# The last stage of an adaLN transformer block: seven block products, three of them 512 columns wide, four accumulated in two banks

## Chip, cores and metric

The kernel runs on one core of a Trainium2 chip. The metric is the device time of one execution in microseconds, as the median of several runs; lower is better.

## What is computed

`x` is 2048 tokens of width D = 512 in float32. The block is a linear-attention layer followed by a bilinear feed-forward layer, each with a layer norm that is scaled and shifted from a conditioning vector. Only the last line of the feed-forward layer is touched by the change.

```python
mod = (silu(c) @ w_mod)                       # sa, ca, ga, sb, cb, gb
h = layernorm(x) * (1 + ca) + sa
x = x + ga * linear_attention(h, wqkv) @ wo   # 32 heads of 16
h = layernorm(x) * (1 + cb) + sb
g = h @ w_gate                                # 512 -> 1376
u = h @ w_up
x = x + gb * ((g * u) @ w_down)               # 1376 -> 512
```

## The kernel before, in words

**Tiles and precision.** Tokens lie in four chunks of 512 (chunk c is `xts[c]`, four tiles of 128 tokens, `j` = 0 to 3). The 1376 features lie in ten tiles of 128 rows and one odd tile of 96. Every float32 operand of a matmul is split in a high part (rounded to the matmul's format, on ScalarE) and a low part (the difference, mostly on VectorE), and a product takes three matmuls: high by high, high by low, low by high.

**The feed-forward layer for chunks 2 and 3.** The generator `ffn` first runs eight gate blocks for chunks 0 and 1 and then eleven for chunks 2 and 3, one per feature tile (order `LATE`: the odd tile first). A gate block (`block`) is seven block products of six 512-column matmuls each (line 1156). Between them stand points named p1, p5, p6, p2, p7, p3, p4, in this order, and a plan (`put(b, point, ...)`) hangs other work on a point of block `m + b`. Block 3 of this numbering begins at 403.49 us in the profile below. Blocks from the fourth on alternate between two sets of four PSUM banks, `banks` and `others`; the last one uses `banks`.

**The last stage.** `Down.run` multiplies the hidden values of chunks 2 and 3 by `w_down`. The ten full feature tiles form five pairs (A, B), and each pair is a 2 by 2 block product done with seven multiplications: a11 and a21 are the hidden values of A for chunks c0 = 2 and c1 = 3, a12 and a22 those of B; b11 and b12 are the left and the right 256 columns of `w_down` for A, b21 and b22 for B. `w_sum` makes t1 to t4 from the b blocks, `h_sum` makes s1 to s4 from the a blocks (s1 = a21 + a22, s3 = a11 - a21, s2 = s1 - a11, s4 = a12 - s2), `h_split` and `h_next` split them. The seven products are a11 b11, s1 t1, a12 b21, s2 t2, s4 b22, s3 t3 and a22 t4. Each goes over all five pairs and over the four token tiles `j`.

The weights are split during the gate blocks, written to DRAM (`w_park`), and fetched again (`w_fetch`, line 1398, on SyncE's DMA queue, five loads of 256 KB for each product). A split weight is one tile of 128 x 2 x 256: high columns, then low columns. The odd feature tile takes no part in the seven products: its 96 rows are added as a plain product of its own, wherever a bank for that output is open.

**What sets the order.** It is written out by hand: each engine executes its instructions in the order in which `run` issues them. SyncE's queue is in order too, so a load that waits for a buffer holds up the loads behind it. All SBUF tiles of 2 KB per partition come from one pool of 94 buffers; `drop` gives the tiles of a finished product back.

**Banks before.** A product is 256 columns wide, so two token tiles share a bank, and a product takes two banks: X = `others[:2]`, Z = `others[2:]`, Y = `banks[:2]`, O = `banks[2:]`. X takes a11 b11; ScalarE copies it to Y (two copies); a12 b21 is then accumulated in X, s2 t2, s3 t3 and a22 t4 in Y, s1 t1 and s4 b22 in Z. `add` lets VectorE add a finished bank to the tokens (line 1503); a bank that is accumulated further is read, not cleared. The products run in halves of two token tiles (`lo`, `hi`), with the preparation of a later product between the halves. The odd tile's right columns for c1 are a short product of their own in O before the last one.

Of the kernel before, what the change touches and what calls it, by code (L numbers as in the profile page):

```python
# [11 lines left out]
ALU = mybir.AluOpType  # L12
AX = mybir.AxisListType

P = 128
# [9 lines left out]
def tile_adaln_block(  # L25
# [12 lines left out]
    nc = tc.nc  # L38
# [4 lines left out]
    NJ = 4  # L43
# [33 lines left out]
    def B(tag, shape=(P, D), dt=F32):  # L77

        return T(tiles, tag, shape, dt)
# [1261 lines left out]

    HALF = D // 2

    FOLLOWS = {"s2": "s4"}

    class Down:

# [59 lines left out]
        def h_sum(self, name, *pairs):  # L1407
            for i in pairs:
                x, y, alu = {"s1": ("a21", "a22", ALU.add), "s3": ("a11", "a21", ALU.subtract),
                             "s2": ("s1", "a11", ALU.subtract), "s4": ("a12", "s2", ALU.subtract)}[name]  # L1410
                own = self.parts.setdefault(i, {})
                x, y = self.a(i, x), self.a(i, y)
                to = {"s1": lambda: B("s"), "s3": lambda: y, "s2": lambda: x, "s4": lambda: x}[name]()
                own[name] = to
                nc.vector.tensor_tensor(to, x, y, op=alu)

# [17 lines left out]
        def ahead(self, name, i):  # L1434
            if name and name not in self.parts[i]:
                self.h_sum(name, i)

        def part(self, bs, j):
            return bs[j // 2][:, j % 2 * HALF:(j % 2 + 1) * HALF]

        def mm(self, bs, j, pairs, start):
# [3 lines left out]
            for n, ((h, l), w) in enumerate(pairs):  # L1445
                k = h.shape[0]
                for x, y in ((h, w[:k, 0]), (h, w[:k, 1]), (l, w[:k, 0])):
                    nc.tensor.matmul(ps, x[:, a:b], y, start=start, stop=False, skip_group_check=True)  # L1448
                    start = False

        def product(self, bs, js, left, right, start, odd=None):
            pairs = [(self.parts[i][left, "split"], self.w[right, i]) for i in range(self.NI)]
            if odd:
                pairs.append((self.h[LATE[0]][odd[0]], self.w["odd", odd[1]]))
            for j in js:
                self.mm(bs, j, pairs, start and j % 2 == 0)

        def drop(self, left, right):
            for i in range(self.NI):
# [2 lines left out]
        def planned(self):  # L1462

            def put(b, point, *does):
                plan.setdefault((self.m + b, point), []).extend(does)

            put(1, "p6", lambda: nc.vector.tensor_tensor(self.odd, self.odd, gb[:self.odd.shape[0]], op=ALU.mult))
            put(1, "p4", *(lambda n=n: self.w_split(("odd", n), self.odd[:, n * HALF:(n + 1) * HALF], nc.gpsimd) for n in range(2)))
            for i in range(self.NI):
                a, b = 1 + 2 * i, 2 + 2 * i  # L1470
                put(a - 1, "p4", lambda i=i: self.w_load(i))
# [15 lines left out]
                if i + 1 < self.NI:  # L1487
                    put(b + 1, "p1", lambda i=i: self.w_park(i, "t2", "t3", "t4"))
                    put(b + 1, "p5", lambda i=i: self.h_sum("s1", i))
                    put(b + 1, "p6", lambda i=i: self.h_sum("s3", i))  # L1490
                else:
                    put(b, "p3", lambda: self.w_fetch("b11"))
                    put(b, "p4", lambda i=i: self.w_park(i, "t2", "t3", "t4"), lambda: self.w_fetch("t1"))

        def run(self):

            c0, c1 = self.cs
            x = lambda c, half, j: xts[c][j][:, half * HALF:(half + 1) * HALF]
            X, Z, Y, O = others[:2], others[2:], banks[:2], banks[2:]

            def add(c, half, bs, js, store=None):
                for j in js:
                    nc.vector.tensor_tensor(x(c, half, j), x(c, half, j), self.part(bs, j), op=ALU.add)
                    if store:
                        a, b = store
                        nc.sync.dma_start(ov[c, j, :, a:b], xts[c][j][:, a:b])

            lo, hi = (0, 1), (2, 3)
            last = self.NI - 1
            self.h_sum("s1", last)  # L1510
            self.h_split("s1", *range(self.NI))
            self.w_fetch("b21")
            self.product(X, lo, "a11", "b11", True)
            copy(Y[0], X[0])
            self.h_split("a12", 0, 1)
            self.product(X, hi, "a11", "b11", True)
            self.h_split("a12", 2)
            copy(Y[1], X[1])
            self.drop("a11", "b11")
            self.h_sum("s3", last)  # L1520
            self.h_split("a12", 3, 4)
            self.w_fetch("t2")
            self.product(Z, lo, "s1", "t1", True)
            self.h_next("s2", 0, 1)
            add(c1, 1, Z, lo)
            self.product(Z, hi, "s1", "t1", True)
            self.h_next("s2", 2, 3)
            add(c1, 1, Z, hi)
            self.drop("s1", "t1")
            self.w_fetch("b22")  # L1530
            self.product(X, lo, "a12", "b21", False, (0, 0))
            self.h_next("s2", 4)
            self.h_next("s4", 0)
            add(c0, 0, X, lo)
            self.product(X, hi, "a12", "b21", False, (0, 0))
            self.h_next("s4", 1, 2)
            add(c0, 0, X, hi)
            self.drop("a12", "b21")
            self.w_fetch("t3")
            self.product(Y, lo, "s2", "t2", False)  # L1540
            self.h_next("s4", 3, 4)
            add(c0, 1, Y, lo)
            self.product(Y, hi, "s2", "t2", False)
            self.h_split("s3", 0, 1)
            add(c0, 1, Y, hi)
            self.drop("s2", "t2")
            self.w_fetch("t4")
            self.product(Z, lo, "s4", "b22", False, (0, 1))
            self.h_split("s3", 2, 3, 4)
            add(c0, 1, Z, lo, (0, D))  # L1550
            self.product(Z, hi, "s4", "b22", False, (0, 1))
            self.h_split("a22", 0, 1)
            add(c0, 1, Z, hi, (0, D))
            self.drop("s4", "b22")
            self.product(Y, lo, "s3", "t3", False)
            self.h_split("a22", 2, 3)
            add(c1, 1, Y, lo)
            self.product(Y, hi, "s3", "t3", False)
            self.h_split("a22", 4)
            add(c1, 1, Y, hi)  # L1560
            self.drop("s3", "t3")
            odd = [(self.h[LATE[0]][1], self.w["odd", 1])]
            for j in range(NJ):
                self.mm(O, j, odd, j % 2 == 0)
            add(c1, 1, O, range(NJ), (HALF, D))
# [5 lines left out]
            add(c1, 0, Y, before, (0, HALF))  # L1571

    def fill(n):
        for _ in range(n):
# [263 lines left out]
```

## Time and profile before

| | |
|---|---|
| median of 3 runs | 541.37 us (541.33 to 541.59) |
| the profiled execution | 541.17 us, of which the span from the first to the last instruction is 539.5 us |
| TensorE | 533.7 us busy, 99% of the span |
| VectorE, ScalarE, GpSimd | 75%, 55%, 30% |
| last stage (479.5 to 535.7 us) | TensorE 56.20 of 56.20 us busy, VectorE 36.59, ScalarE 15.94, GpSimd 0; granted TensorE clock 1.00 |
| after the last matmul | one add on VectorE, one store of 128 KB |

The profile is one execution. In it, a matmul's record begins when the matmul starts and ends by a model, so records overlap and the distance from one start to the next is what a matmul costs; "PEld" is the loading of a matmul's stationary weights, which has records of its own. In this kernel each matmul has its own load. "L1448 PE" names a line of the program and the engine. The chain of waits is followed back from the last instruction.

### The profile page before, as it was taken

To read this page: it belongs to the slowest core of one execution; us is meant where nothing else is said; L and a number is where in the kernel's file an instruction comes from. 1 tells how busy PE (TensorE), PEld (TensorE's weight loads), DVE (VectorE), ACT (ScalarE), POOL (GpSimd) and SP (SyncE) were. 2 spreads that over 40 slices of the span, in tenths; PEclk is the share of its full clock that TensorE was granted. 3 is DMA by queue.
4 is the path that set the end of the run, shared out by engine and by line. 5 is a ranking of instruction groups with operands and counts; after the bars stand their busy time and mean duration, and the time that the engine had idled before them with its cause. 6 is when DMAs were issued, how large, how long until landed. Compare 5 with 4: busy or idle time off the path is not lost.

```text
span 539.5 us, 8146 instructions
## 1 busy us (share of the span) xinstructions
PE 533.7 (99%) x2617; PEld 447.8 (83%) x2617; DVE 402.6 (75%) x688; ACT 295.8 (55%) x557; POOL 159.5 (30%) x169
## 2 busy tenths in 40 slices
PE   8999999999999999999999999999999999999997
PEld 6888787888888878878888888887888888899997
DVE  7997779999989888779766576996555564669742
ACT  3696777648587764577684545454434334264500
POOL 2001010010021220076696577747532313210000
PEclk9999999999999999999999999999999999999999
DMA  8913426220165165947879596793289998689222
GB/s 279 386 37 102 133 94 219 88 69 2 37 203 187 47 207 145 311 138 225 283 208 320 194 329 217 223 378 105 81 297 346 393 393 305 221 300 346 91 80 78
DMA packets 86394, 109.20 MB, mean 202 GB/s; under 512 B 10896, under 2 KB 41616, under 8 KB 86352
## 3 DMA queue, kind: packets, MB, share of 16 engines
q1 hardware_dynamic: 86352, 108.70, 59.6%
q8 instruction: 20, 0.33, 0.2%
q14 instruction: 22, 0.18, 0.1%
HBM read 65.93 MB, written 42.73 MB: 201 GB/s over the span
## 4 chain that ended last, share of the span: by engine, by line
PE 94%; DVE 3%; SPq 1%; issue 1%; DMA 0%; ACT 0%; DVEq 0%
PE bank L1156 27%; PE acc L873 8%; PE acc L1156 7%; PE acc L1448 6%; PE bank L1448 5%; PE bank L211 4%; PE bank L209 3%; PE bank L210 3%; PE acc L1239 3%; PE acc L1240 3%; PE acc L1241 3%; PE acc L416 2%; PE acc L418 2%; PE bank L956 2%; PE bank L958 2%; PE acc L417 2%
## 5 line engine op out<-in xcount | busy, mean ns | idle before, releaser
L1156 PE MATMUL bank<-h,w 128*128 128x512 f32 (+1 forms) x630 | 145.3, 389 | 0.0
L1156 PEld LDWEIGHTS bank<-h,w 128*128 128x128 f32 (+1 forms) x630 | 117.1, 186 | 25.9
L1161 ACT ACTIVATE bank<-bank 128x512 f32<-128x512 f32 (+1 forms) x30 | 17.5, 584 | 74.5 <-PE bank L1156 74.4
L197 DVE TENSOR_TENSOR kl<-u,kh 128x512 fp32r<-128x512 f32 (+1 forms) x38 | 26.5, 735 | 25.4 <-ACT kh L196 23.3
L265 POOL TENSOR_TENSOR rstd<-ve,half 128x2 f32<-128x2 f32 (+3 forms) x13 | 11.8, 910 | 108.6 <-DVE ve L264 44.0
L211 PE MATMUL bank<-w,h 128*128 128x512 f32 x104 | 40.9, 393 | 0.1
L209 PE MATMUL bank<-w,h 128*128 128x512 f32 x104 | 40.9, 393 | 0.0
L210 PE MATMUL bank<-w,h 128*128 128x512 f32 x104 | 40.5, 390 | 0.0
L1156 PE MATMUL acc<-h,w 128*128 128x512 f32 x168 | 38.7, 389 | 0.0
L197 POOL TENSOR_TENSOR w<-raw,w 128x512 fp32r<-128x512 f32 (+1 forms) x15 | 22.1, 1479 | 53.4 <-ACT w L196 47.8
L873 PE MATMUL acc<-w,xh 128*128 128x512 f32 x120 | 37.1, 390 | 0.0
L1156 PEld LDWEIGHTS acc<-h,w 128*128 128x128 f32 x168 | 31.5, 188 | 6.5
L943 DVE TENSOR_TENSOR x<-acc,x 128x512 f32<-128x512 f32 x40 | 26.5, 686 | 12.8 <-PE acc L1241 11.1
L1118 POOL TENSOR_TENSOR w<-raw,w 128x256 fp32r<-128x256 f32 (+3 forms) x22 | 24.4, 1108 | 37.8 <-ACT w L1111 33.6
L1448 PE MATMUL acc<-w,kh 128*128 128x256 f32 (+1 forms) x176 | 31.8, 283 | 0.0
L1118 POOL TENSOR_TENSOR w<-t,w 128x512 fp32r<-128x512 f32 (+1 forms) x22 | 29.7, 1350 | 0.0
L1448 PEld LDWEIGHTS acc<-w,kh 128*128 128x128 f32 (+1 forms) x176 | 27.5, 192 | 0.1
L873 PEld LDWEIGHTS acc<-w,xh 128*128 128x128 f32 x120 | 22.5, 188 | 4.6
L416 PE MATMUL acc<-kh,xh 128*128 128x512 f32 x64 | 25.2, 394 | 0.0
L418 PE MATMUL acc<-kl,xh 128*128 128x512 f32 x64 | 25.0, 391 | 0.0
L417 PE MATMUL acc<-kh,xl 128*128 128x512 f32 x64 | 25.0, 390 | 0.0
L1239 PE MATMUL acc<-w,kh 128*128 128x512 f32 x64 | 24.9, 389 | 0.0
(261 smaller groups left out, 1325.8 us busy)
## 6 DMA issues: line engine op xcount, KB each, us to landing
right<-w SPq DMA_DIRECT2D x56, 256.0 KB, 3.5
w<-right SPq DMA_DIRECT2D x56, 256.0 KB, 5.1
raw<-in_w_mod_dram SPq DMA_DIRECT2D x24, 256.0 KB, 3.8
raw<-in_B_w_down_dram SPq DMA_DIRECT2D x20, 256.0 KB, 3.8
down_t<-w SPq DMA_DIRECT2D x20, 256.0 KB, 5.0
w<-down_t SPq DMA_DIRECT2D x20, 256.0 KB, 4.6
x<-in_A_x_dram SPq DMA_DIRECT2D x16, 256.0 KB, 5.4
down_b<-w SPq DMA_DIRECT2D x15, 256.0 KB, 5.1
```

The source lines that it names most:

```text
L197: (low or nc.vector).tensor_tensor(l, src, f32(h), op=ALU.subtract)
L209: nc.tensor.matmul(ps, ah, bh, start=i == 0, stop=False)
L210: nc.tensor.matmul(ps, ah, bl, start=False, stop=False)
L211: nc.tensor.matmul(ps, al, bh, start=False, stop=i == n - 1)
L416: nc.tensor.matmul(tacc[k], xh[:, a:b], kh, start=first, stop=False)
L417: nc.tensor.matmul(tacc[k], xl[:, a:b], kh, start=False, stop=False)
L418: nc.tensor.matmul(tacc[k], xh[:, a:b], kl, start=False, stop=last)
L873: nc.tensor.matmul(yps[i], x, y, start=False, stop=k == KD - 1 and x is al, skip_group_check=True)
L1118: sub = lambda out, x, y: (on or nc.gpsimd).tensor_tensor(out, x, f32(y), op=ALU.subtract)
L1156: mm = lambda x, y, **kw: nc.tensor.matmul(ps, x[:, k], y, skip_group_check=True, **kw)
L1239: nc.tensor.matmul(ps, hh[:, a:b], dh[:n, c:d], start=i == 0, stop=False)
L1448: nc.tensor.matmul(ps, x[:, a:b], y, start=start, stop=False, skip_group_check=True)
```

## The change

In the last stage, products are now of two kinds. **Wide**: a12 b21, s1 t1 and s4 b22 use all four banks A = `banks`, one per token tile. The high part of `a` is multiplied by the weight's high and low columns side by side, 512 columns in one matmul, and the low part by the high 256 columns, which are accumulated on the left half of the bank: two matmuls where there were three. VectorE then adds the left and the right half of each bank to the tokens. **Narrow**: a11 b11, s2 t2, s3 t3 and a22 t4 are accumulated one after the other in C = `others[:2]`, 256 columns at a time as before, and VectorE adds the running sum to another quarter of the output after each. The two copies from X to Y are gone.

The two kinds alternate: a11 b11 (C), a12 b21 (A), s2 t2 (C), s1 t1 (A), s3 t3 (C), s4 b22 (A), a22 t4 (C). Products run whole, no longer in halves. The odd tile's right columns for c1 are put into the chain with s3 t3; since they then also stand in what follows, the last product adds the odd tile with its left minus its right columns. `odd_turn`, at point p5 of block 3, makes this difference in place (a VectorE subtraction, a ScalarE copy, a GpSimd subtraction, each 96 x 256). s2 is now written over a11 and not over s1, which is split later; s1's and s3's last sums both stand before the first product.

```diff
-    FOLLOWS = {"s2": "s4"}
+    FOLLOWS = {}
...
-                to = {"s1": lambda: B("s"), "s3": lambda: y, "s2": lambda: x, "s4": lambda: x}[name]()
+                to = {"s1": lambda: B("s"), "s3": lambda: y, "s2": lambda: y, "s4": lambda: x}[name]()
...
+        def odd_turn(self):
+            x = self.odd
+            nc.vector.tensor_tensor(x[:, :HALF], x[:, :HALF], x[:, HALF:], op=ALU.subtract)
+            self.w_split(("odd", "turn"), x[:, :HALF], nc.gpsimd)
...
+        def mm_wide(self, bs, j, pairs, start):
+
+            a, b = j * P, (j + 1) * P
+            for (h, l), w in pairs:
+                k = h.shape[0]
+                nc.tensor.matmul(bs[j], h[:, a:b], w[:k].rearrange("p t c -> p (t c)"), start=start, stop=False, skip_group_check=True)
+                nc.tensor.matmul(bs[j][:, :HALF], l[:, a:b], w[:k, 0], start=False, stop=False, skip_group_check=True)
+                start = False
...
+            put(3, "p5", self.odd_turn)
...
-                    put(b, "p4", lambda i=i: self.w_park(i, "t2", "t3", "t4"), lambda: self.w_fetch("t1"))
+                    put(b, "p4", lambda i=i: self.w_park(i, "t2", "t3", "t4"), lambda: self.w_fetch("b21"))
...
+            A, C = banks, others[:2]
...
-                    nc.vector.tensor_tensor(x(c, half, j), x(c, half, j), self.part(bs, j), op=ALU.add)
+                    parts = [bs[j][:, :HALF], bs[j][:, HALF:]] if bs is A else [self.part(bs, j)]
+                    for ps in parts:
+                        nc.vector.tensor_tensor(x(c, half, j), x(c, half, j), ps, op=ALU.add)
...
+            self.h_sum("s1", last)
+            self.h_sum("s3", last)
+            self.h_split("a12", *pairs)
+            self.w_fetch("t2")
+            self.product(C, js, "a11", "b11", True)
+            self.drop("a11", "b11")
+            self.h_next("s2", 0, 1)
+            add(c0, 0, C, js)
+            self.w_fetch("t1")
+            self.product(A, js, "a12", "b21", True, (0, 0))
+            self.drop("a12", "b21")
+            self.h_next("s2", 2, 3, 4)
+            add(c0, 0, A, js)
+            self.w_fetch("t3")
+            self.product(C, js, "s2", "t2", False)
+            self.drop("s2", "t2")
+            self.h_split("s1", *pairs)
+            add(c0, 1, C, js)
+            self.w_fetch("b22")
+            self.product(A, js, "s1", "t1", True)
+            self.drop("s1", "t1")
+            self.h_split("s3", *pairs)
+            self.h_next("s4", 0)
+            add(c1, 1, A, js)
+            self.w_fetch("t4")
+            self.product(C, js, "s3", "t3", False, (1, 1))
+            self.drop("s3", "t3")
+            self.h_next("s4", 1, 2, 3, 4)
+            add(c1, 1, C, js, (HALF, D))
+            self.product(A, js, "s4", "b22", False, (0, 1))
+            self.drop("s4", "b22")
+            self.h_split("a22", *pairs)
+            add(c0, 1, A, js, (0, D))
...
-                self.product(Y, (j,), "a22", "t4", False, (1, 0))
-                add(c1, 0, Y, before, (0, HALF))
+                self.product(C, (j,), "a22", "t4", False, (1, "turn"))
+                add(c1, 0, C, before, (0, HALF))
```

**Order on TensorE, at the end of the stage's first product.** In the program before, the second product is s1 t1 in Z (`acc_4525`); `w` is a weight tile, `kh` and `kl` the high and low part of a hidden value (here the stationary operand is the hidden value, whatever the order of the names); x2 is two matmuls that read alike, by the high and by the low columns.

```order
L1448 MATMUL acc_4524<-w_5254,kh_5199 128x256 x2
L1448 MATMUL acc_4524<-w_5254,kl_5200 128x256
L1448 MATMUL acc_4525<-w_5269,kh_5281 128x256 x2
L1448 MATMUL acc_4525<-w_5269,kl_5282 128x256
L1448 MATMUL acc_4525<-w_5271,kh_5285 128x256 x2
L1448 MATMUL acc_4525<-w_5271,kl_5286 128x256
```

The same place in the changed program; the second product is a12 b21 in A (`bank_2865` for the first token tile).

```order
L1453 MATMUL acc_4524<-w_5258,kh_5203 128x256 x2
L1453 MATMUL acc_4524<-w_5258,kl_5204 128x256
L1461 MATMUL bank_2865<-w_5273,kh_5286 128x512
L1462 MATMUL bank_2865<-w_5273,kl_5287 128x256
L1461 MATMUL bank_2865<-w_5275,kh_5290 128x512
L1462 MATMUL bank_2865<-w_5275,kl_5291 128x256
```

The first product is as before; in the second, each group of three matmuls of 256 columns has become one of 512 and one of 256.

**Order on SyncE's DMA queue, at the start of the stage.** These are the loads for the second and the third product before: t1, then b21 (the number behind the block's name is the pair).

```order
L1398 DMA w_1113_5271<-down_t1_1_4682 128x512
L1398 DMA w_1114_5273<-down_t1_2_4868 128x512
L1398 DMA w_1115_5275<-down_t1_3_5054 128x512
L1398 DMA w_1116_5277<-down_t1_4_5226 128x512
L1398 DMA w_1128_5301<-down_b21_0_4495 128x512
L1398 DMA w_1129_5303<-down_b21_1_4645 128x512
```

And in the changed program, at the same places of the queue:

```order
L1398 DMA w_1114_5275<-down_b21_1_4649 128x512
L1398 DMA w_1115_5277<-down_b21_2_4835 128x512
L1398 DMA w_1116_5279<-down_b21_3_5021 128x512
L1398 DMA w_1117_5281<-down_b21_4_5193 128x512
L1398 DMA w_1129_5306<-down_t2_0_4548 128x512
L1398 DMA w_1130_5308<-down_t2_1_4738 128x512
```

The loads are as many and as large; their order is now b21, t2, t1, t3, b22, t4, the order in which the products need them, where it was t1, b21, t2, b22, t3, t4.

**Order on VectorE, between the last gate block and the second product.** Before: the last multiplication of the gate block (L1184), the last s1 sum (L1415), then the low parts of s1 (L197, `kl`).

```order
L1184 TENSOR_TENSOR u_5197<-bank_2867,u_5197 128x512
L1415 TENSOR_TENSOR s_5279<-u_5120,u_5197 128x512
L197 TENSOR_TENSOR kl_5282<-s_4564,kh_5281 128x512
L197 TENSOR_TENSOR kl_5286<-s_4750,kh_5285 128x512
L197 TENSOR_TENSOR kl_5290<-s_4936,kh_5289 128x512
```

After: the last s3 sum stands there too, and the low parts are those of a12.

```order
L1184 TENSOR_TENSOR u_5201<-bank_2867,u_5201 128x512
L1415 TENSOR_TENSOR s_5283<-u_5124,u_5201 128x512
L1415 TENSOR_TENSOR u_5124<-u_5135,u_5124 128x512
L197 TENSOR_TENSOR kl_5287<-u_4442,kh_5286 128x512
L197 TENSOR_TENSOR kl_5291<-u_4670,kh_5290 128x512
```

The five low parts that the second product needs moved back by one sum.

More of the change, by code (lines that the diff above doesn't have):

```diff
@@ L1455, in product @@
             for j in js:
-                self.mm(bs, j, pairs, start and j % 2 == 0)
+                if len(bs) == NJ:
+                    self.mm_wide(bs, j, pairs, start)
+                else:
+                    self.mm(bs, j, pairs, start and j % 2 == 0)
         def drop(self, left, right):
@@ L1506, in add @@
                         nc.sync.dma_start(ov[c, j, :, a:b], xts[c][j][:, a:b])
-            lo, hi = (0, 1), (2, 3)
+            lo, hi, js = (0, 1), (2, 3), range(NJ)
+            pairs = range(self.NI)
             last = self.NI - 1
             self.h_sum("s1", last)
[L1511 to L1516, printed above, removed]
@@ L1517, in run @@
-            self.h_split("a12", 2)
-            copy(Y[1], X[1])
+            self.h_sum("s3", last)
+            self.h_split("a12", *pairs)
+            self.w_fetch("t2")
+            self.product(C, js, "a11", "b11", True)
             self.drop("a11", "b11")
[L1520 to L1523, printed above, removed]
             self.h_next("s2", 0, 1)
-            add(c1, 1, Z, lo)
-            self.product(Z, hi, "s1", "t1", True)
@@ L1527, in run @@
-            self.h_next("s2", 2, 3)
-            add(c1, 1, Z, hi)
+            add(c0, 0, C, js)
[10 more added lines that the diff above has]
+            self.w_fetch("b22")
@@ L1540, in run @@
[L1540 to L1546, printed above, removed]
-            self.w_fetch("t4")
[L1548 to L1551, printed above, removed]
@@ L1552, in run @@
-            self.h_split("a22", 0, 1)
-            add(c0, 1, Z, hi, (0, D))
-            self.drop("s4", "b22")
[L1555 to L1564, printed above, removed]
@@ L1570, in run @@
                 before = (j,)
-            add(c1, 0, Y, before, (0, HALF))
+            add(c1, 0, C, before, (0, HALF))
     def fill(n):
```

11 lines of the change are left out of this document (removed).

## The prediction

> **What bounds the kernel now.** I read the page's head first, then the chain of waits in order of time for the last 110 us, then the timeline of TensorE where the last stage begins. The head says which engine is full, the chain whether anything else ever ends last.
>
> ```profile
> span 539.5 us, 8146 instructions
> PE 533.7 (99%) x2617; PEld 447.8 (83%) x2617; DVE 402.6 (75%) x688; ACT 295.8 (55%) x557; POOL 159.5 (30%) x169
> ...
> 470.13 9.52 PE bank L1156 x42
> 479.65 23.03 PE acc L1448 x192
> 502.68 7.20 PE bank L1448 x60
> 509.88 8.64 PE acc L1448 x72
> 518.52 17.29 PE bank L1448 x144
> 535.81 0.02 issue
> 535.84 0.42 DVE x L1503
> ```
>
> From 470 us to the end the chain is TensorE alone, then one VectorE add and the last store. A 512-column matmul costs 9.52 / 42 = 0.2267 us. The last stage is 192 + 60 + 72 + 144 = 468 matmuls of 256 columns in 23.03 + 7.20 + 8.64 + 17.29 = 56.16 us, 0.120 us each, with no gap between the pieces. So the stage is bound by TensorE's instruction stream, and a term counts if it shortens that stream or makes it wait.
>
> Why do 256 columns cost more than half of 512? The starts at the border between the two sizes tell (timeline of TensorE: start, us, then the instruction).
>
> ```profile
> 479.26 0.39 PE L1156 MATMUL bank<-h,w 128*128 128x512 f32 x1
> 479.49 0.28 PE L1448 MATMUL acc<-w,kh 128*128 128x256 f32 x1
> 479.60 0.28 PE L1448 MATMUL acc<-w,kh 128*128 128x256 f32 x1
> 479.72 0.28 PE L1448 MATMUL acc<-w,kl 128*128 128x256 f32 x1
> 479.84 0.28 PE L1448 MATMUL acc<-w,kh 128*128 128x256 f32 x1
> ```
>
> The 512-column matmul takes 0.23. The first of 256 columns behind it takes 0.11, the next ones 0.12. Half of 0.2267 is 0.1133, so the first goes at the price of its columns, and the steady 0.120 must have another limit. The stage where 256 and 128 columns alternate names it:
>
> ```profile
> 130.80 0.34 PE L809 MATMUL acc<-w,w 128*128 128x256 f32 x1
> 130.97 0.22 PE L810 MATMUL acc<-w,w 128*128 128x128 f32 x1
> 131.03 0.34 PE L809 MATMUL acc<-w,w 128*128 128x256 f32 x1
> 131.21 0.22 PE L810 MATMUL acc<-w,w 128*128 128x128 f32 x1
> ```
>
> There 128 columns take 0.06, again half of 0.113, but the pair takes 131.03 - 130.80 = 0.23 where its columns come to 0.17: two weight loads of 0.115 set it. A weight load thus lasts 0.115 to 0.120, and a stream of narrow matmuls runs at the pace of its loads, one of 512 columns at that of its columns.
>
> **The change: TensorE.** Each group of three narrow matmuls costs 3 x 0.120 = 0.360. In a wide product it becomes one of 512 columns (0.2267) and one of 256 behind it. That second one stands as the one at 479.49 does, behind a 512-column matmul that has hidden its load, so I take 0.1133 and 0.340 for the group; its two loads need 0.24 and are hidden. The upper end is the steady 0.120, 0.3467 for the group. Neither matmul can go below the price of its columns, so 0.340 is also the lower end.
>
> There are 3 wide products x 5 pairs x 4 token tiles = 60 groups, and two of them carry the odd tile, 4 groups each: 68. The 12 matmuls of the odd product in O move into the chain, 12 for 12. Count: 468 = 264 that stay narrow + 68 x 3. Saving: 68 x 0.020 = 1.36 us, at the upper end 68 x 0.0133 = 0.91 us.
>
> The upper end is also what a fixed price per matmul would give: a line through 0.2267 and 0.120 has 0.1067 for 256 columns and 0.0133 for the instruction, and the change takes one instruction out of each group. The Trainium skill has such a rule, and it speaks against the change: "TensorE: Matmul & The Clock Gate", section "Back-to-back issue gap", gives columns / 2.4 GHz + 2.5 ns, by which, as an estimate, only 68 x 2.5 ns = 0.17 us would be saved. The trace disagrees in both sizes (0.2267 where the rule gives 0.216, 0.120 where it gives 0.109); the same section's other statement, that load and matmul set the spacing together, is what the rows show.
>
> **The change: what could make TensorE wait.** With the new prices the products start at 479.49 (C), 486.69 (A), 494.85 (C), 502.05 (A), 508.85 (C), 517.49 (A) and 525.65 (C), and end at 534.29 instead of 535.65.
>
> VectorE first. It gets 40 adds of 256 columns for 28, and one sum ahead of the splits of the second product.
>
> ```profile
> 480.49 0.69 DVE L1415 TENSOR_TENSOR s<-u,u 128x512 f32<-128x512 f32 x1
> 481.10 3.09 DVE L197 TENSOR_TENSOR kl<-s,kh 128x512 fp32r<-128x512 f32 x5
> L1503 DVE TENSOR_TENSOR x<-x,bank 128x256 f32<-128x256 f32 x16 | 6.1, 419 | 13.0 <-PE bank L1448 13.0
> L1503 DVE TENSOR_TENSOR x<-x,acc 128x256 f32<-128x256 f32 x12 | 4.5, 416 | 5.1 <-PE acc L1448 5.1
> ```
>
> A sum takes a step of 0.61 (481.10 - 480.49), so the fifth low part of a12 ends at 484.8 instead of 484.2; the second product first wants it behind four groups, at 488.1. Twelve more adds are 12 x 0.42 = 5.0 us in a stage where VectorE idled 18.1 us for TensorE. The adds of an A bank must be done before that bank is written again, a narrow product (7.2 us) later; they take 8 x 0.42 = 3.4 us, most of it while the product still runs. C is read within 1.7 us behind each narrow product and written again only after a wide one (6.8 us or more). All of this is hidden, and I cost it at nothing; without the cover each late microsecond would be one on TensorE. In the last product the second token tile of a bank waits until the first one's add is done, as before (529.36 below is such an add, it ended 1.7 us before it was wanted); the last of the wide adds, in front of it now, end 0.8 us after the product before, and the first tile itself takes 18 x 0.12 = 2.16. The two ScalarE copies that go had nobody waiting.
>
> Then the weights. SyncE's rows, and the landing times of the five t1 loads at 478.29, whose place b21 takes:
>
> ```profile
> 478.29 2.33 SPq L1398 DMA_DIRECT2D w<-down_t  x5
> 480.72 2.31 SPq L1398 DMA_DIRECT2D w<-down_b  x5
> 483.12 3.16 SPq L1398 DMA_DIRECT2D w<-down_t  x5
> 486.67 3.04 SPq L1398 DMA_DIRECT2D w<-down_b  x5
> 492.63 8.51 SPq L1398 DMA_DIRECT2D w<-down_t  x10
> ...
> DMA to landing us min/median/max: 2.7/3.8/4.6
> ```
>
> The last of the five is issued at 480.2 and lands by 484.8, 3.3 us before the second product wants it. Each later load keeps its place within the queue, and its product comes at nearly the old time, so I cost the loads at nothing too.
>
> The odd tile's difference adds a ScalarE copy in block 3, between two copies of which TensorE waits for the second.
>
> ```profile
> 403.49 9.52 PE acc L1156 x42
> 404.13 1.29 DVE L1368 TENSOR_TENSOR raw<-raw,row 128x512 f32<-128x512 f32 x2
> 406.25 0.60 ACT L1161 ACTIVATE u<-acc 128x512 f32<-128x512 f32 x1 [0.78 <-PE acc L1156]
> 407.61 0.58 ACT L1161 ACTIVATE acc<-acc 128x512 f32<-128x512 f32 x1 [0.76 <-PE acc L1156]
> 409.07 2.13 POOL L1360 TENSOR_TENSOR w<-raw,w 128x256 fp32r<-128x256 f32 x3 [8.53 <-ACT w L1359]
> ```
>
> The subtraction follows the scaling, 405.4 to 405.8 (the price of a 256-column add), the copy fits in ScalarE's idle 0.76 before 407.61, GpSimd idles 8.53. Cost nothing; the cover ends about 0.6 us later, since the fifth product of the block starts at 403.49 + 24 x 0.2267 = 408.93 and needs the copy, which ends at 408.19. The extra buffer moves the pool's turn by one, so later loads wait for a neighbour of the matmul that they waited for.
>
> Last, the end. The four 256 KB stores for c0 now lie in the last product, the 128 KB ones for c1 before them.
>
> ```profile
> out_dram<-x SPq DMA_DIRECT2D x4, 256.0 KB, 2.9
> ...
> 529.36 0.42 DVE L1503 TENSOR_TENSOR x<-x,bank 128x256 f32<-128x256 f32 x1 [1.41 <-PE bank L1448]
> ...
> 536.28 0.33 SPq L1506 DMA_DIRECT2D out_dram<-x  x1
> ```
>
> The last of them is issued at about 526.5 and lands 2.9 us later, the final store is issued at 534.9: no effect. The tail behind the last matmul stays as it is.
>
> **Sum.** On the profiled execution, 541.17 - 1.36 = 539.81; it lies 0.20 under the median of the runs, so 541.37 - 1.36 = 540.01 us, 0.25% less. What a measurement of this kernel can tell from no change is 0.2%, 1.08 us.
>
> **Rivals.**
>
> *Only a fixed price per matmul is saved*, the narrow one staying at 0.120 beside a wide one (540.46 us, within 0.2%). For it: the mean over all 468 before is 0.120. Against it: the one step with the same neighbour in front is 0.11, and 128 columns go in 0.06, where the line has 0.067. Chance 0.15. (With the skill's smaller fixed part it would be 541.2 us, on the same side of the bound.)
>
> *Weights come late* (slower). Place: the start of a wide or a chained product, where TensorE's first matmul with a pair waits for its load; price: each microsecond late is one of TensorE's. For it: the queue is in order and loads wait for buffers given back by products that now run whole instead of in halves. Against it: no row of before shows TensorE waiting for such a load, and the least spare time, at the second product, is 3.3 us. It decides from there: to end slower by over 0.2% a load must be late by 1.36 + 1.08 = 2.4 us on TensorE, so land 5.7 us later than t1 did; with two products hit by 1.5 us each the time is 541.37 - 1.36 + 3.0 = 543.0. Chance 0.07.
>
> *A small wait eats part of it* (540.4 to 541.6, within 0.2%): block 3's copy late by 1 us, say, is 0.4 us on TensorE. Chance 0.07.
>
> **How the numbers follow.** The forecast itself has 0.71. The range 539.7 to 540.8 holds it with the spread of the runs (0.26 us) and some of its roundings, the narrow rival, and the smaller of the small waits; it leaves out the rest, about 0.15. Faster by over 0.2% is the forecast less a little for 540.01 lying only 0.28 us beyond the bound: 0.69. Within 0.2%: 0.15 + 0.07 + 0.02 = 0.24. Slower: 0.07.
>
> **What would show it.** In the profile after: 332 narrow and 68 wide matmuls in the stage; starts 0.227 and 0.113 apart in turn within a wide product (0.120 would be the narrow rival); the chain from 479.65 on TensorE alone, 54.80 us long in place of 56.16; no idle time of TensorE put down to a load (line 1398), a split or an add; block 3 still 9.52. I am wrong if the wide groups cost more than 0.347, or if a product starts later than in the list above.

## The result and the profile after

The changed kernel takes 540.49 us (539.95 to 540.93, 14 runs) where the kernel before takes 541.57 us (541.02 to 542.08, 14 runs): ratio 0.9981, 95% interval 0.9973 to 0.9988. That is 1.08 us less, with an interval of 0.65 to 1.46 us. Forecast were 1.36 us. The measured 0.19% lies just inside the 0.2% that the prediction took for no change, the case to which it gave a chance of 0.24. The profile shows that the 1.08 us are a sum of other terms than the forecast's.

The page's head and the chain of waits of the changed kernel (start us, us, engine, tile, line, count):

```profile
span 538.2 us, 8020 instructions
PE 532.7 (99%) x2549; PEld 443.6 (82%) x2549; DVE 408.8 (76%) x701; ACT 295.1 (55%) x556; POOL 160.2 (30%) x170
```

```profile
469.85 9.52 PE bank L1156 x42
479.37 7.19 PE acc L1453 x60
486.57 0.23 PE bank L1461
...
494.99 7.18 PE acc L1453 x60
502.17 0.23 PE bank L1461
...
509.25 8.63 PE acc L1453 x72
517.88 0.23 PE bank L1461
...
526.30 8.63 PE acc L1453 x72
534.96 0.42 DVE x L1523
```

As forecast, the chain is TensorE alone from before the stage to the last add. Narrow products cost 0.120 us per matmul (7.19 / 60). The wide ones last 494.99 - 486.57 = 8.42, 509.25 - 502.17 = 7.08 and 526.30 - 517.88 = 8.42 us, 23.92 us for 68 groups: **0.352 us per group**, not 0.340. The timeline of TensorE, at the start of the second product and in its third token tile (start us, us, instruction):

```profile
486.40 0.40 PE L1461 MATMUL bank<-w,kh 128*128 128x512 f32 x1
486.64 0.28 PE L1462 MATMUL bank<-w,kl 128*128 128x256 f32 x1
486.75 0.40 PE L1461 MATMUL bank<-w,kh 128*128 128x512 f32 x1
487.00 0.28 PE L1462 MATMUL bank<-w,kl 128*128 128x256 f32 x1
487.12 0.40 PE L1461 MATMUL bank<-w,kh 128*128 128x512 f32 x1
...
491.34 0.39 PE L1461 MATMUL bank<-w,kh 128*128 128x512 f32 x1
491.57 0.28 PE L1462 MATMUL bank<-w,kl 128*128 128x256 f32 x1
491.69 0.39 PE L1461 MATMUL bank<-w,kh 128*128 128x512 f32 x1
```

The narrow step behind a wide one is 0.11 to 0.12, so it does get cheaper than 0.120. But the 512-column step, 0.2267 among its own kind, is 0.23 to 0.24 here. The two together take 0.35 (491.69 - 491.34) to 0.37 (487.12 - 486.75); the starts shown are rounded to 0.01 us.

The ends of the stage, from the same view, of the changed kernel (first two rows) and of the kernel before (third):

```profile
479.21 0.40 PE L1453 MATMUL acc<-w,kh 128*128 128x256 f32 x2
...
534.64 0.28 PE L1453 MATMUL acc<-w,kl 96*128 96x256 f32 x1
```

```profile
535.52 0.28 PE L1448 MATMUL bank<-w,kl 96*128 96x256 f32 x1
```

From its first matmul's start to its last one's, the stage took 535.52 - 479.49 = 56.03 us before and takes 534.64 - 479.21 = 55.43 us now: 0.60 us less. The spans, 539.46 and 538.23 us before rounding, differ by 1.23 us. Another 0.28 is ahead of the stage (479.49 to 479.21), and 0.35 behind the last matmul: up to the start of the trace's last record, the end takes 3.53 us instead of 3.89. The prediction had "the tail stays as it is". The experiments show which of the three terms are the change's.

### The profile page after: what moved, and what is told of

Its sections match the earlier page's. It is cut to its first block, busy times and chain, and to the rows that moved or that the text cites. A ratio compares the mean times of both kernels' runs of the same rounds, so it can differ in the third digit from the quotient of the medians.

```text
span 538.2 us, 8020 instructions
## 1 busy us (share of the span) xinstructions
PE 532.7 (99%) x2549; PEld 443.6 (82%) x2549; DVE 408.8 (76%) x701; ACT 295.1 (55%) x556; POOL 160.2 (30%) x170
## 4 chain that ended last, share of the span: by engine, by line
PE 92%; DVE 4%; DMA 1%; issue 1%; SPq 1%; ACT 0%; POOL 0%; DVEq 0%; POOLq 0%
PE bank L1156 27%; PE acc L873 8%; PE acc L1156 7%; PE acc L1453 6%; PE bank L211 4%; PE bank L209 3%; PE bank L210 3%; PE bank L1461 3%; PE acc L1239 3%; PE acc L1240 3%; PE acc L1241 3%; PE acc L416 2%; PE bank L958 2%; PE bank L956 2%; PE acc L418 2%; PE acc L417 2%
## 5 line engine op out<-in xcount | busy, mean ns | idle before, releaser
L197 DVE TENSOR_TENSOR kl<-u,kh 128x512 fp32r<-128x512 f32 (+1 forms) x38 | 26.7, 749 | 23.9 <-ACT kh L196 21.9
L197 POOL TENSOR_TENSOR w<-raw,w 128x512 fp32r<-128x512 f32 (+1 forms) x15 | 22.2, 1484 | 53.4 <-ACT w L196 47.8
```

Of the source, the lines that this page charges most:

```text
L197: (low or nc.vector).tensor_tensor(l, src, f32(h), op=ALU.subtract)
```

## The experiments

"Stage" is from the first to the last matmul start of the last stage, "end" from there to the start of the trace's last record; both come from one profile each. The time is the median beside that of the kernel before on the same chip.

| kernel | stage us | end us | time us, beside before | ratio, 95% interval |
|---|---|---|---|---|
| before | 56.03 | 3.89 | | |
| changed | 55.43 | 3.53 | 540.49, 541.57 | 0.9981 (0.9973 to 0.9988) |
| A narrow again | 56.03 | 3.53 | 541.22, 541.51 | 0.9995 (0.9987 to 1.0004) |
| wide first, then narrow | 55.49 | 3.53 | 540.53, 541.51 | 0.9981 (0.9972 to 0.9990) |
| six wide | 54.58 | 3.53 | 539.78, 541.51 | 0.9969 (0.9956 to 0.9981) |
| six wide, once more | 54.58 | 3.53 | 539.84, 541.63 | 0.9970 (0.9959 to 0.9982) |
| last product wide too | 54.38 | 3.54 | 539.65, 541.63 | 0.9968 (0.9955 to 0.9980) |
| before + odd difference | 56.03 | 3.89 | 541.78, 541.84 | 0.9998 (0.9989 to 1.0007) |
| before + difference + 1 | 56.03 | 3.54 | 541.33, 541.63 | 0.9996 (0.9987 to 1.0005) |
| changed, low on VectorE | 55.43 | 3.88 | 540.92, 541.84 | 0.9985 (0.9976 to 0.9994) |
| changed, b21 late | 55.82 | 3.53 | 540.44 (one run) | |

### Is it the wide form?

```diff
-                nc.tensor.matmul(bs[j], h[:, a:b], w[:k].rearrange("p t c -> p (t c)"), ...)
-                nc.tensor.matmul(bs[j][:, :HALF], l[:, a:b], w[:k, 0], ...)
+                for x, y in ((h, w[:k, 0]), (h, w[:k, 1]), (l, w[:k, 0])):
+                    nc.tensor.matmul(bs[j][:, :HALF], x[:, a:b], y, ...)
```

> The changed order, banks, odd tile in the chain and VectorE program stay, but the three products in A are done with three 256-column matmuls per group again (all into the left half of a bank, one add per token tile). It separates the wide form from everything else that the change moves. If the wide form alone gives what the last stage gained (68 groups x about 8.5 ns = 0.6 us in the profile after), the stage is 468 x 0.120 = 56.16 us again and what is left of the gain is what lies outside the stage: 541.0 to 541.3 us if the shorter end behind the last store (0.3 us) belongs to the changed program, 541.5 if that was chance. Rival, the order and the banks gave the gain: 540.5 to 540.8 us.

The second product in this kernel's chain of waits:

```profile
487.28 8.64 PE bank L1462 x72
```

8.64 / 72 = 0.120, and the stage is back at 56.03. Order, banks and the odd tile in the chain give the stage nothing; its 0.60 us are the wide form's. The shorter end stayed, and the 0.29 us of the time fit it, though the interval of the ratio holds 1.

### What does a matmul cost?

```diff
+            for n in range(40):
+                nc.tensor.matmul(U, at(n)[0], at(n)[3], ...)              # 512; then 384, 320, 256, 192, 128
+            for n in range(80):
+                nc.tensor.matmul(U[:, :(512, 256)[n % 2]], at(n // 2)[n % 2], at(n // 2)[3][:, :(512, 256)[n % 2]], ...)
...
```

> Behind the last product of the changed kernel stand extra matmuls into two free banks, with the last product's operands, one stream per source line: 40 each of 512, 384, 320, 256, 192 and 128 columns, then 80 each in mixed orders (512/256 in turn into one bank; the same into two banks; two and two; five and five; 512/128 in turn), then 40 of 256. Steps by theory. Load pace (the forecast: the longer of 0.443 ns per column and a load of 0.115 to 0.120): 0.227, 0.170, 0.142, 0.120, 0.118, 0.118; mixed 0.340 per pair in turn, 0.3467 two and two and five and five, 512/128 0.342. Fixed price (0.0133 us and 0.417 ns per column): 0.227, 0.173, 0.147, 0.120, 0.093, 0.067; mixed 0.347 in every order, 512/128 0.293. Fixed price with a load that needs its 0.117: the first four as by the fixed price, then 0.117 twice; mixed 0.347, 512/128 0.344. Price of the alternation itself, as the profile after suggests (0.352 per group): 0.350 to 0.355 in turn, 0.347 to 0.350 two and two, 0.347 five and five; if two accumulations of different width in one bank are its reason, 0.347 in two banks.

Its chain of waits, one piece per stream in the order of the text above:

```profile
535.70 9.09 PE acc L1581 x40
544.79 6.96 PE acc L1583 x40
551.75 5.86 PE acc L1585 x40
557.61 4.79 PE acc L1587 x40
562.41 4.45 PE acc L1589 x40
566.85 4.44 PE acc L1591 x40
571.29 13.92 PE acc L1593 x80
585.21 13.87 PE acc L1595 x80
599.08 13.94 PE acc L1597 x80
613.02 14.03 PE acc L1599 x80
627.05 13.56 PE acc L1601 x80
```

Us per matmul, or per pair where two widths alternate, beside what two of the rules give:

| columns | measured | fixed price | load pace |
|---|---|---|---|
| 384 | 0.174 | 0.173 | 0.170 |
| 320 | 0.1465 | 0.1467 | 0.142 |
| 192 | 0.111 | 0.093 | 0.115 to 0.120 |
| 128 | 0.111 | 0.067 | 0.115 to 0.120 |
| 512 and 256 in turn | 0.348, 0.347 | 0.347 | 0.340 |
| 512 and 128 in turn | 0.339 | 0.293 | 0.342 |

384 and 320 columns decide it: they lie on the line through 512 and 256, that is 0.417 ns per column and a fixed 0.0133 us per matmul, and off the forecast's line. Only below 256 columns is there another limit, and it is 0.111 at 192 and at 128 columns alike, not 0.120. It may be the weight load; no run has narrow matmuls with other loads, so that is not shown. 512 and 128 in turn are near the sum of the two prices, 0.2267 + 0.111 = 0.338. In turn, 512 and 256 cost 0.347, in one bank or in two; two and two 0.3485, five and five 0.351. The price of the alternation that the profile after suggested is not there in these streams, and the banks don't matter.

### Does the order inside a group matter?

```diff
             for (h, l), w in pairs:
...
-                nc.tensor.matmul(bs[j][:, :HALF], l[:, a:b], w[:k, 0], ...)
                 start = False
+            for (h, l), w in pairs:
+                nc.tensor.matmul(bs[j][:, :HALF], l[:, a:b], w[:k, 0], ...)
```

> Only the order inside a wide product's token tile is changed: first its five or six 512-column matmuls, then its five or six of 256 columns. If the alternation costs the 5 ns by which a group lies above 0.3467, the group falls from 0.352 to 0.347 and the kernel gains 68 x 5 ns = 0.34 us on the changed one (about 540.15 us). By the forecast's own rule, narrow matmuls behind narrow ones would lose the hidden load: 0.3467 too, which is then a loss against its 0.340, but the profile after has shown no 0.340. If the 5 ns belong to the operands of these products and not to the order, 512 columns stay at 0.235 and 256 go back to 0.120: 0.355, 0.2 us slower than the changed kernel (540.7 us).

The stage is 55.49, the same as the changed kernel's within 0.06 us, and so is the time. Neither the gain nor the loss came; 68 groups save 0.55 us, so one costs 0.352 here too, near to the five and five of the streams (0.351).

### Why 0.352 in the kernel and 0.347 in the streams?

```diff
+            for n in range(40):
+                nc.tensor.matmul(U[:, :256], ...)                          # entry: 40 of 256 columns
+            for n in range(80):
+                nc.tensor.matmul(U[:, :(512, 256)[n % 2]], ...)            # 40 groups
...
```

> Extra matmuls behind the last product of the changed kernel again, one stream per line. It asks why a wide group costs 0.354 in some products and 0.347 in the streams that alternated before. Streams of 40 groups of 512 and 256 columns: entered from 40 matmuls of 256 columns; from 40 of 512; from 256 with the narrow one of each group first; from 256 with one matmul of 128 columns between; from 256 with one group on 96 rows of the odd tile in the middle. Then pairs of 512 and 192, 512 and 288, 384 and 256. If the state in which a stream is entered decides (a group of 0.347 or 0.353 that keeps itself up), the first two are at 0.353, the one behind 128 columns at 0.347, and the one with 96 rows changes in its middle. If the work of the other engines beside it decides, which is gone here, all are at 0.347. Fixed price with a load of 0.111: 512/192 0.338, 512/288 0.360, 384/256 0.293; the forecast's load pace: 0.338 to 0.342, 0.354, 0.283.

The pieces of its chain of waits: groups behind 256 columns (L1586), behind 512 (L1590), narrow first (L1594), behind one of 128 (L1600), behind the group on 96 rows (L1608), then the pairs of 512/192, 512/288 and 384/256:

```profile
540.31 14.13 PE acc L1586 x80
...
563.57 14.12 PE acc L1590 x80
...
582.49 14.13 PE acc L1594 x80
...
601.49 14.19 PE acc L1600 x80
...
627.90 14.13 PE acc L1608 x80
642.02 13.75 PE acc L1610 x80
655.77 14.57 PE acc L1612 x80
670.34 11.72 PE acc L1614 x80
```

With no other engine at work beside them, groups entered from a narrow or a wide stream cost 14.13 / 40 = 0.353; so the other engines' work is not the reason. One matmul of 128 columns ahead does not bring 0.347 (0.355), nor does a group on 96 rows (0.353); 40 of 128 columns, which stood ahead of the streams at 0.347, were not tried again. So there are two steady states, 0.347 and 0.353, that keep themselves up for 40 groups, and my guess at what switches them fell. In the changed kernel the second product starts at 0.355 in its first token tile and is at 0.349 in its third and fourth, s1 t1 stays at 0.352 to 0.354. Six wide products, run twice (below), gave 54.58 us both times, so the program sets the state and not chance. What picks the state stays open. 384/256 at 0.293 is the fixed price again (0.2933; load pace 0.283); 512/288 (0.364) lies 4 ns above it, and 512/192 (0.344) 6 ns above 0.2267 + 0.111.

### More of the wide form

```diff
-            A, C = banks, others[:2]
+            A, C = banks, others
...
-                if len(bs) == NJ:
-                    self.mm_wide(bs, j, pairs, start)
+                if left == "a22":
+                    self.mm(bs, j, pairs, False)                # on the left halves
                 else:
-                    self.mm(bs, j, pairs, start and j % 2 == 0)
+                    self.mm_wide(bs, j, pairs, start)
...
             self.h_split("a22", *pairs)
+            add(c1, 0, C, js, None, (1,))      # the right halves, ahead of the last product
```

> The wide form for six of the seven products: the chain runs in four banks, its first three products wide as well, and the last one narrow on the left halves; the right halves are added by VectorE before it, so the end keeps one 256-column add. 60 + 4 more groups are wide, 132 in all. If the gain of the wide form is 8.5 ns per group as in the profile after, this gives 64 x 8.5 ns = 0.54 us on the changed kernel (about 539.95 us) as long as VectorE's 16 more adds (6.7 us) stay hidden. By the forecast's 20 ns it would be 1.28 us (539.2). If the gain came from elsewhere than the wide form: 540.5 us or slower.

132 groups: 1.45 us less in the stage than before, 11.0 ns per group, and 1.73 us less in the time. That is more than the 8.5 ns of the profile after and far from 20: the 64 further groups took 55.43 - 54.58 = 0.85 us out, 13.3 ns each, the fixed price of one matmul. So over all 132 a group costs 0.349, and it is not the same in every place. VectorE's 16 more adds took none of this away.

> The kernel with six wide products once more, beside the others: its stage should be 54.58 us again if the steps of 0.347 and 0.353 are set by the program and not by chance, and the time 0.3% under before.

54.58 us once more, to the hundredth. Then the last product wide for its first three token tiles:

```diff
-                if left == "a22":
+                if left == "a22" and j == 3:
                     self.mm(bs, j, pairs, False)
...
-            add(c1, 0, C, js, None, (1,))
+            add(c1, 0, C, (3,), None, (1,))
```

> Six wide products as before in this study, and the last product wide too for its first three token tiles; the fourth stays narrow, so that one 256-column add is left at the end. 3 x 6 = 18 more wide groups at 0.349 instead of 0.360: 0.2 us less than with six, stage 54.38 us after 54.58. If VectorE's extra adds or the banks' reads hold the last product up, the gain is lost and TensorE shows idle time for VectorE there.

The timeline of TensorE, first and last matmul of the stage:

```profile
479.63 0.39 PE L1461 MATMUL acc<-w,kh 128*128 128x512 f32 x1
...
534.01 0.28 PE L1453 MATMUL acc<-w,kl 96*128 96x256 f32 x1
```

534.01 - 479.63 = 54.38, as expected. It has the shortest stage of the study; its 539.65 us are 0.3% under the kernel before (ratio 0.9968, 0.9955 to 0.9980). Against six wide, the 0.2 us show in the stage and are too few for the times.

### The end

```diff
+            put(3, "p5", self.odd_turn)        # in the kernel before; its result is not used
```

> The kernel before with one thing of the change alone: the odd tile's difference in block 3 (one VectorE subtraction, one ScalarE copy, one GpSimd subtraction); the result is not used. Two questions. Block 3: by the forecast it stays at 9.52 us. The end: from the last matmul's start to the end of the span it was 3.89 us before, and 3.53 in the changed kernel and in each of its variants so far; before's records show an instruction fetch on the DMA queue in this stretch, the others none. If GpSimd's one more instruction moves where its closing instructions are fetched, the end is 3.53 here too and the time 541.15 to 541.25 us (0.3 less than before). Rival, the end is shorter for what stands in the last product (stores, banks): 3.89 and 541.5 us.

The stretch from 538 us on, DMA queues (packets, MB, share), of the kernel before; the changed kernel has no such row there:

```profile
q14 instruction: 1, 0.01, 0.6%
```

The end stayed at 3.89 us, and this kernel has the fetch too. This did not settle the count of instructions: beside the one added subtraction one of GpSimd's waits fell away, so that its records in the trace are 330 as before (331 in the changed kernel). So the opposite was tried, and then one instruction more.

```diff
-            self.w_split(("odd", "turn"), x[:, :HALF], nc.gpsimd)
+            self.w_split(("odd", "turn"), x[:, :HALF])
```

> The changed kernel with the low part of the odd tile's difference on VectorE, so GpSimd has as many instructions as before the change. If GpSimd's count of instructions sets the shorter end, the end goes back from 3.53 to 3.89 us, an instruction fetch stands in it, and the kernel takes 540.8 us (0.3 more than the changed one). Rival, the end belongs to the last product: 3.53 us and 540.5 us.

GpSimd's records are 330, and the end is 3.88 us with an instruction fetch behind it, while the stage is still 55.43: the end is not the last product's. The time (0.92 us under before, interval 0.33 to 1.30) is too coarse to tell 0.60 from 0.95.

```diff
             self.w_split(("odd", "turn"), x[:, :HALF], nc.gpsimd)
+            nc.gpsimd.memset(x[:, :1], 0.0)
```

> The kernel before with the odd tile's difference and one GpSimd instruction more, a memset of one column of a tile that nobody reads again. In the records of GpSimd (waits included) the runs with the long end, 3.89 us, have 330 (before; before with the odd tile's difference, where one wait fell away; the changed kernel with the low part on VectorE), those with the short end, 3.53 us, have 331. If the count alone decides, this one has 331, its end is 3.53 us without an instruction fetch, and the time is 0.35 us under before with the stage at 56.03 us. Rival, the end belongs to the new last stage: 3.89 us, no change.

331 records, no fetch, 3.54 us, with the old last stage (56.03). So in two pairs of kernels one GpSimd instruction, a subtraction in one pair and a memset in the other, sets the end. The 0.30 us in the time agree, though the interval of the ratio holds 1. In every profiled execution the time is the span and 1.7 us, so a shorter end is a shorter time.

By the trace's times the fetch is not what the end waited for: it starts at 539.56 us in the kernel before, 0.10 us after the last record has ended, and 0.06 to 0.07 after it in the other two. The longer part is GpSimd's own, its closing records of the kernel before (first two rows) and of the changed one (ns min/median/max, first and last start):

```profile
L1833 POOLq EVENT_SEMAPHORE  x4: 17/17/17, 538.4 to 539.4; - x4
L1833 POOLq DRAIN  x3: 34/128/1634, 476.3 to 539.2; - x3
```

```profile
L1831 POOLq EVENT_SEMAPHORE  x4: 17/17/17, 537.6 to 538.1; - x4
L1831 POOLq DRAIN  x3: 34/78/1632, 476.0 to 538.0; - x3
```

Unrounded, these four semaphore records span 0.92 us before and 0.57 now, which is the whole 0.35: 0.30 of it lie between the first and the second, 0.05 in a drain (128 ns, now 78). Up to the first of them the two ends agree within 0.01 us. In place of the late fetch, all ten traces with 331 records, the two kernels with added streams among them, have an 8 KB fetch at 479.4 to 480.5 us, 1.8 to 1.9 us after GpSimd's last calculation. That GpSimd's 0.30 us are a wait for instructions is likely, but no row shows it.

### The cover of b21

```diff
-                    put(b, "p4", ..., lambda: self.w_fetch("b21"))
+                    put(b, "p4", ..., lambda: self.w_fetch("t2"))
...
-            self.w_fetch("t2")
+            self.w_fetch("b21")
```

> The changed kernel with the loads of b21 and of t2 in the old order on the queue: t2's five first, b21's five behind them. It takes away 2.4 us of the cover that the prediction gave b21. In the changed kernel b21's loads are issued from 477.98 to 480.36 us and t2's from 480.45 on; a load there lands 4.2 to 5.4 us behind its issue. Behind t2's, b21's five are issued from 480.45 to 482.8 and land from 485 to 488.2, where the second product wants its first pair at 486.4 and its fifth at 487.8. If the cover is 3.3 us as forecast, TensorE idles 0 to 0.4 us for a load in the second product's first token tile and nowhere else. Rival, the loads were never near the edge: no idle time. Rival, each late load moves all behind it: over 1 us.

SyncE's queue, then TensorE's weight loads in the second product (in brackets the idle time before):

```profile
478.10 2.74 SPq L1398 DMA_DIRECT2D w<-down_t  x5
480.90 2.32 SPq L1398 DMA_DIRECT2D w<-down_b  x5
...
487.59 0.19 PEld L1461 LDWEIGHTS bank<-w,kh 128*128 128x128 f32 x1 [0.15 <-issue]
...
488.25 0.19 PEld L1461 LDWEIGHTS bank<-w,kh 128*128 128x128 f32 x1 [0.37 <-ACT kh L1429]
```

Only the fourth and the fifth pair waited, 0.15 and 0.37 us, and the stage grew by 0.39 us to 55.82. (The row names a copy for s2, which this product doesn't use; only the loads were moved, and so the fifth of them is what was late.) In the trace the fourth and the fifth load land at 487.48 and 488.15, 0.1 us before the weight loads that waited. In the changed kernel the fifth lands at 484.75, and its matmul starts at 487.81: a cover of 3.06 us. It lands 3.40 us later here, 2.92 of them by its later issue (480.90 against 477.98), so 0.34 are missing, near the 0.37 of the row.

## Why the prediction was right or wrong

**The price of a group: wrong.** The step that failed is "a weight load thus lasts 0.115 to 0.120, and a stream of narrow matmuls runs at the pace of its loads". The pace below 256 columns is 0.111 (192 and 128 columns), whether it is the load's or not; 0.120 is the price of 256 columns themselves, and 0.0133 us of it is paid per matmul at every width from 256 to 512 (320 and 384 columns). So a wide group saves that fixed part at most: 0.3467, the rival that had a chance of 0.15. I had ruled it out on one step, 0.11 at 479.49, and on the 0.06 of 128 columns. Both are real, but a short step has a longer neighbour: in the changed kernel the narrow steps are 0.11 to 0.12 and the wide ones 0.23 to 0.24; with 512 and 128 in turn the pair is 0.339 however short the narrow step. The pair of 256 and 128 columns that the prediction read as two loads, 0.23, is also 0.120 + 0.111. "Neither matmul can go below the price of its columns" took half of 0.2267 for that price. The prediction's own signs of being wrong came true: a group costs more than 0.347, and the products start later.

**The size: 0.60 us of the stage instead of 1.36.** At 0.3467 the 68 groups would have saved 0.91; at the measured 0.352 they save 68 x 0.0083 = 0.56, and the rest of the 0.60 are narrow steps next to the wide products. The term of the sum that was mis-sized is 0.020 us per group, which measured 0.008.

The Trainium skill's rule, "TensorE: Matmul & The Clock Gate", section "Back-to-back issue gap", stated there for an isolated matmul, has the right form, a price per column and one per instruction. Its 2.5 ns per instruction are 13 in the streams here. The trace agrees with its price per column.

**The tail: wrong, in the other direction.** "The tail behind the last matmul stays as it is" named the add and the store and left out the closing instructions of the engines. GpSimd's one more instruction made its closing part 0.35 us shorter; why is open. Stage and end give 0.60 + 0.35 = 0.95 us, inside the measured 0.65 to 1.46, and the same sum lies near most other kernels: 0.35 for 0.29 (A narrow), 0.90 for 0.98 (wide first), 1.81 for 1.73 and 1.79 (six wide), 2.00 for 1.98 (last product wide), 0 for 0.06 and 0.35 for 0.30 (before, without and with one more). It is farthest off where the changed kernel has the long end: 0.60 for 0.92, inside that interval too.

**The span: chance.** The 0.28 us ahead of the stage are not the change's: eight kernels with the same program up to there began the stage at 479.21 to 480.33 us. The spans' difference of 1.23 us is thus three terms, one of them luck, and its likeness to 1.36 proves nothing. The median landed near the forecast because the missing 0.76 us of the stage were about half made up by a term that the prediction did not have; that too is luck.

**Covers: right.** TensorE waits for nothing in the stage. VectorE's twelve adds more are hidden:

```profile
479.50:535.00 55.50, 55.42 (x399) 52.16 (x398) 41.23 (x84) 14.71 (x26) 0.00 (x0) 1.00 0.49 177
```

(The columns are us, then busy time of TensorE, its weight loads, VectorE, ScalarE, GpSimd, then the clock, the DMA share and GB/s.) VectorE went from 36.59 to 41.23 us. b21's loads are issued from 477.98 on; their cover of about 3 us is what the experiment used up. Block 3 with the odd tile's copy, in the chain and in ScalarE's timeline:

```profile
403.21 9.52 PE acc L1156 x42
```

```profile
406.47 0.40 ACT L1359 ACTIVATE w<-raw 96x256 fp32r<-96x256 f32 x1
407.33 0.58 ACT L1161 ACTIVATE acc<-acc 128x512 f32<-128x512 f32 x1 [0.46 <-PE acc L1156]
```

It is 9.52 us as before, and ScalarE still idled 0.46 us ahead of the copy that TensorE needs. The count holds too: 60 + 8 matmuls of 512 columns and 332 narrow ones. The products' starts do not hold: with the first at 479.21 (forecast 479.49), the last starts at 526.14 where 525.65 was forecast, 0.77 us later by the length of the stage.

**The rivals.** *Only a fixed price* was the right one for the price of a matmul. *Weights come late* and *a small wait* did not occur.

## What to carry to other kernels

A price read from one short step at a border is not a price: take the mean over a repeating group, and where two rules give the same number at the widths in the trace, measure a third width. Fusing two matmuls of 256 columns saves the fixed part of one (0.0133 us here, less what an uneven stream gives back) and no more. Below that width there is more to save: by the streams, two of 128 columns cost 2 x 0.111 and one of 256 costs 0.120, an estimate that no kernel here tried. When the total agrees with the forecast, still compare stage by stage: here it agreed because an unrelated 0.35 us at the end stood in for part of a missing 0.76.

## What was unexpected of the hardware

One instruction more on an engine made the kernel's end shorter: with 330 records of GpSimd (three kernels) the end takes 3.88 to 3.89 us, and an 8 KB instruction fetch starts 0.06 to 0.10 us after it; with 331 (the other rows of the table) the end takes 3.53 to 3.54, and a fetch of this size stands at 479.4 to 480.5 us instead. The Trainium skill, "Runtime: NRT & Kernel Launch", section "Instruction fetch mechanics", says that an engine's instructions are fetched ahead in blocks. The trace agrees in that one instruction more moves a fetch by some 60 us; what GpSimd's closing records wait for stays open.

A stream of 512 and 256 columns in turn has two steady prices, 0.347 and 0.353 us per pair, with nothing else at work. Each held for 40 pairs; what switches between them is open.
